# Attention with the keys on the partitions and no row maximum, ahead of a mixture of depths

## The chip, the cores and the metric

The kernel runs on one core of a Trainium2 chip. A core has a matrix engine (TensorE, PE in the rows, with its weight loads as PEld), three engines for elementwise work (VectorE or DVE, ScalarE or ACT, GpSimd or POOL), a queue engine (SyncE or SP) and 16 DMA engines. The metric is the device time of the program in microseconds (us), the median of several runs. All data is float32, for which each matmul of the program is carried out in two passes of the matrix engine; a transpose takes one.

## What is computed

```python
q_n, k_n = rmsnorm(q, g_q), rmsnorm(k, g_k)          # q, k, v: (8, 12, 448, 64)
scores = matmul(q_n, k_n.transpose(0, 1, 3, 2)) / sqrt(64)
attn = exp(scores - max(scores)); attn = attn / (sum(attn) + 1e-9)
x = matmul(attn, v).transpose(0, 2, 1, 3).reshape(8, 448, 768)
# mixture of depths: per batch, the 128 tokens with the highest x @ w_gate
out = x; out[top] += sigmoid(x[top] @ w_gate) * (relu(x[top] @ w1) @ w2)   # w1: 768 x 1024
```

## The kernel before

A batch has 448 tokens; token 4 p + j lies on partition p (112 of them) at place j. The work is cut into units: batch, pair of heads c (six per batch), block j of 112 queries, 192 units in all; four heads are a group, whose q, k and v are loaded three groups ahead (L72, one SP queue). `normalize` (L131) squares a group's q and k on POOL, sums on DVE, takes the power -1/2 on POOL (L144) and scales q and k on POOL (L152). `transpose_pair` (L162) turns q and k of two heads on PE (L170) and multiplies them with g on DVE and ACT.

`scores` (L187) multiplies one block of queries with all keys, queries on the partitions, for two heads whose 64 dims lie on the lower and upper half of the partitions (L193); DVE takes the row maximum from the result (L201), ACT the exponential with its row sum (L206). `transpose_probs` (L216) turns each head's probabilities block by block on PE (L222) and copies them out on DVE and ACT. `values` (L237) multiplies them, now keys on the partitions, with v: the probabilities are the stationary operand and v with its 64 columns the moving one, four blocks of keys per head (L245). DVE divides by the row sums and writes x (L255).

`mixture` (L265) is a generator that yields after each piece. Its pieces run between the units of the next batch: the gate's scores (L276), each token's rank by comparison with all others (L304, L314), a one-hot selection (L354), the gather of the chosen rows by matmuls (L368), the products with w1 (L400) and w2 (L420), and a scattered addition into the output (L433). The mixture of the last batch runs alone at the end.

The loop at L446 sets the order: at step i the scores of unit i, the transposes of unit i - 1, the values of unit i - 2, and one piece of the mixture. The framework's scheduler then orders each engine's queue, and each engine takes its queue strictly in order.

## Time and profile before

| | us |
|---|---|
| median of 3 runs | 1139.58 |
| lowest and highest run | 1129.56, 1142.35 |
| span of the profiled execution | 1137.9 |
| PE busy | 1009.8 (89%) |
| PE weight loads busy | 795.4 (70%) |
| DVE busy | 619.0 (54%) |
| ACT busy | 396.2 (35%) |
| POOL busy | 335.3 (29%) |

The page shows one profiled execution. Matmuls are pipelined, so PE's busy share is not a measure of how near it is to its limit; the spacing of starts in the timeline is. The granted clock is that of PE, 1.00 for 2.4 GHz throughout a stretch.

### The profile page before, as it was taken

The page shows a single profiled execution, that of the slowest core. Times are in us where ns is not written, and L with a number is a line of the kernel's source. Part 1 is how long each engine was busy: PE and PEld are TensorE (multiplying, and loading weights), DVE is VectorE, ACT ScalarE, POOL GpSimd, SP SyncE. Part 2 cuts the span into 40 slices and gives each one's busy share as a digit, 9 for nine tenths or more (in the row PEclk, how much of TensorE's full clock was granted, in tenths as well). Part 3 has the DMA queues.
Part 4 walks back from the last instruction along what each step waited for, and adds up shares of the span by engine and source line. Part 5 has one row for each costly group of instructions (what it writes and reads, how often), then busy time and mean ns, then how long its engine had stood idle before and what let it go on. Part 6 is the DMA issues. An engine that isn't in the chain of part 4 may idle for free.

```text
span 1137.9 us, 17977 instructions
## 1 busy us (share of the span) xinstructions
PE 1009.8 (89%) x7264; PEld 795.4 (70%) x7264; DVE 619.0 (54%) x1379; ACT 396.2 (35%) x1049; POOL 335.3 (29%) x165
## 2 busy tenths in 40 slices
...
DMA packets 37938, 54.98 MB, mean 48 GB/s; under 512 B 1776, under 2 KB 34032, under 8 KB 36960
## 3 DMA queue, kind: packets, MB, share of 16 engines
q1 hardware_dynamic: 36384, 50.68, 15.6%
...
q8 instruction: 58, 0.95, 0.3%
q14 instruction: 24, 0.20, 0.1%
...
## 4 chain that ended last, share of the span: by engine, by line
PE 67%; POOL 21%; DVE 5%; issue 4%; DMA 1%; ACT 1%; POOLq 0%; SPq 0%; ACTq 0%
PE av L245 23%; PE sc L193 13%; PE pt_ps L222 13%; POOL rinv L144 10%; PE moe_ps L420 6%; PE moe_ps L400 4%; POOL sq L138 4%; PE qk_ps L170 4%; PE moe_ps L368 3%; POOL qn L152 3%; POOL kn L152 3%; DVE ss L139 2%; DVE nmax L201 2%; DMA q<-in_q_dram 1%; ACT p L206 1%
## 5 line engine op out<-in xcount | busy, mean ns | idle before, releaser
L245 PE MATMUL av<-v,pt 112*112 112x64 f32 x3072 | 368.7, 276 | 33.6 <-DVE x L255 33.6
L245 PEld LDWEIGHTS av<-v,pt 112*112 112x112 f32 x3072 | 358.1, 195 | 35.4 <-DVE x L255 35.4
L201 DVE TENSOR_REDUCE nmax<-sc 112x2 f32<-112x896 f32 x192 | 208.2, 1085 | 164.3 <-PE sc L193 164.3
L206 ACT ACTIVATE p<-sc,nmax 112x448 f32<-112x448 f32 x384 | 240.0, 632 | 150.4 <-DVE nmax L201 148.1
L222 PEld LDWEIGHTS pt_ps<-ident,p 112*112 112x112 f32 x1536 | 161.6, 143 | 161.5 <-ACT p L206 83.2
L222 PE MATMUL pt_ps<-ident,p 112*112 112x112 f32 x1536 | 207.6, 279 | 48.8 <-ACT p L206 43.0
L231 ACT COPY pt<-pt_ps 112x448 f32<-112x448 f32 x192 | 102.2, 532 | 339.8 <-PE pt_ps L222 339.8
L193 PE MATMUL sc<-kT,qT 64*112 64x448 f32 x768 | 217.2, 642 | 0.0
L229 DVE COPY pt<-pt_ps 112x448 f32<-112x448 f32 x192 | 118.3, 616 | 44.3 <-PE pt_ps L222 44.3
L144 POOL TENSOR_TENSOR rinv<-ss,neg_half 112x32 f32<-112x32 f32 x24 | 134.1, 5589 | 1.6
L152 POOL TENSOR_TENSOR qn<-q,rinv 112x1024 f32<-112x1024 f32 x24 | 49.1, 2046 | 266.8 <-PE qk_ps L170 266.7
L139 DVE TENSOR_REDUCE ss<-sq 112x16 f32<-112x1024 f32 x48 | 58.3, 1215 | 123.8 <-POOL sq L138 123.8
L433 POOL DMA_INDIRECT out_dram<-y,row x8 | 13.1, 1633 | 374.3 <-DVE y L429 374.3
L255 DVE TENSOR_TENSOR x<-av,rden 112x128 f32<-112x128 f32 x192 | 55.6, 289 | 89.8 <-PE av L245 88.9
L400 PE MATMUL moe_ps<-xeT,w 128*128 128x128 f32 x768 | 94.0, 280 | 0.9 <-ACT hT L409 0.7
L400 PEld LDWEIGHTS moe_ps<-xeT,w 128*128 128x128 f32 x768 | 89.8, 195 | 1.2 <-ACT hT L409 0.9
L420 PE MATMUL moe_ps<-w,hT 128*128 128x384 f32 x256 | 89.2, 493 | 1.4 <-DVE y L429 0.7
L193 PEld LDWEIGHTS sc<-kT,qT 64*112 64x112 f32 x768 | 58.1, 187 | 31.5 <-issue 16.7
L206 ACT ACTIVATION_READ_ACCUMULATOR p<-sc,nmax 112x1 f32 x384 | 77.4, 202 | 0.0
L181 ACT ACTIVATE kT<-qk_ps,gk 128x448 f32<-128x448 f32 x48 | 30.4, 633 | 134.0 <-PE qk_ps L170 134.0
L170 PEld LDWEIGHTS qk_ps<-ident,qn 112*128 112x128 f32 x192 | 22.7, 163 | 62.2 <-issue 32.4
L420 PEld LDWEIGHTS moe_ps<-w,hT 128*128 128x128 f32 x256 | 46.3, 190 | 28.2 <-DVE y L429 1.3
...
## 6 DMA issues: line engine op xcount, KB each, us to landing
q<-in_q_dram SPq DMA_DIRECT2D x24, 448.0 KB, 4.4
k<-in_k_dram SPq DMA_DIRECT2D x24, 448.0 KB, 6.7
v<-in_v_dram SPq DMA_DIRECT2D x24, 448.0 KB, 5.8
...
out_dram<-y,row POOLq DMA_INDIRECT x8, 5.6
gq<-in_g_q_dram ACTq DMA_DIRECT2D x2, 0.2 KB, 5.1
```

Source lines behind the costliest of these rows:

```text
L139: nc.vector.tensor_reduce(out=ss[:, i], in_=sq, axis=AX.X, op=OP.add)
L144: nc.gpsimd.tensor_tensor(out=rinv.rearrange(flat), in0=ss.rearrange(flat), in1=neg_half.to_broadcast([CP, 2 * GH * NJ]), op=OP.pow,)
L152: nc.gpsimd.tensor_tensor(out=t.rearrange("p j h d -> p h j d"), in0=loaded.pop((nm, n)), in1=rinv[:, i, :, :, None].to_broadcast([CP, GH, ...
L193: nc.tensor.matmul(out=sc[:, hh, 0:S], lhsT=qT[r, CP * j : CP * (j + 1)], rhs=kT[r, :], start=True, stop=True,)
L201: nc.vector.tensor_reduce(out=nmax, in_=sc[:, :, 0:S], axis=AX.X, op=OP.max, negate=True)
L206: nc.scalar.activation(out=p, in_=sc[:, hh, 0:S], func=AF.Exp, bias=nmax[:, hh : hh + 1], accum_out=den[:, hh : hh + 1],)
L222: nc.tensor.transpose(out=pt_ps[:CP, kc, :], in_=ps[hh][:, CP * kc : CP * (kc + 1)], identity=ident[:CP, :CP],)
L229: nc.vector.tensor_copy(out=pt, in_=pt_ps[:CP])
L231: nc.scalar.copy(out=pt, in_=pt_ps[:CP])
L245: nc.tensor.matmul(out=av[:, hh, :], lhsT=pts[hh][:, kc, :], rhs=loaded["v", b * NG + 2 * c // GH][:, 2 * c % GH + hh, kc, :], start=(kc = ...
L400: nc.tensor.matmul(out=ps[:, 128 * i : 128 * i + n], lhsT=w1[:, dc, 128 * (f0 + i) : 128 * (f0 + i + 1)], rhs=xeT[:, dc, :n], start=(dc == 0),
L420: nc.tensor.matmul(out=ps[:n, : DM // 2], lhsT=hT[:, fc, :n], rhs=w2[:, fc, cols], start=(fc == 0), stop=(fc == NFC - 1),)
```

## The change

The old program becomes the function `general`. A test on the chip forms the largest square of g_q times g_k; if it is at most 3600/64 a branch takes the new function `fast`, else `general`. With rows of q and k divided by their rms, scores can't exceed 60 in that case, so `fast` takes the exponential of the scores without a maximum.

In `fast` the host hands q and k over transposed as well (dims on the partitions), v and the tokens in the order of the partitions. The sum of squares is formed from the token copies (square on ACT, sum on DVE, power on POOL). The factor of k's rows is the scale of the exponential, since keys are on the partitions; the factors of q's rows are stored to DRAM as rows and loaded again onto all partitions (`rows`, `bc`), and `scale_q` multiplies them with q and both g's on DVE.

A unit is now two heads and one block of 112 keys. `scores` gives keys on the partitions and all 448 queries in the columns. `values` uses v as the stationary operand (64 columns for each head, written to the lower or upper 64 partitions of one bank) and the probabilities as the moving one; four units add up to x of two heads, transposed. The sums over keys are added up on DVE (`add_probs`) and finished by four matmuls with ones per group, and x and the sums are turned on PE (`finish_group`). The mixture's pieces are the same; it starts eight units after its batch's end, and the last one runs at the end. `y` has one buffer in place of two.

```diff
+    def load_tokens(n):
+        b, h0 = n // NG, n % NG * GH
+        for i in range(2):
+            t = load_pool.tile([CP, GH, NJ, D], F32, name="tok", bufs=4)
+            nc.sync.dma_start(out=t, in_=tok[b, :, i, h0 : h0 + GH])
+            toks[n, i] = t
+    def load_group(n):
+        b, g = n // NG, n % NG
+        for store, src, name in ((qTs, qT, "qT"), (kTs, kT, "kT")):
+            t = load_pool.tile([128, GH // 2, S], F32, name=name, bufs=2 if name == "qT" else 3)
+            nc.sync.dma_start(
+                out=t, in_=src[b, g * GH // 2 : (g + 1) * GH // 2].rearrange("c p s -> p c s")
+            )
+            store[n] = t
+        t = load_pool.tile([CP, GH, NJ, D], F32, name="v")
+        nc.sync.dma_start(out=t, in_=vp[b, :, g * GH : (g + 1) * GH])
+        vs[n] = t
...
+    def inverse_rms(n):
+        ss = norm_pool.tile([CP, 2, GH, NJ], F32, name="ss")
+        for i in range(2):
+            t = toks.pop((n, i))
+            sq = norm_pool.tile([CP, GH, NJ, D], F32, name="sq", bufs=1)
+            nc.scalar.activation(out=sq, in_=t, func=AF.Square)
+            nc.vector.tensor_reduce(out=ss[:, i], in_=sq, axis=AX.X, op=OP.add)
+            yield
+        rinv = norm_pool.tile([CP, 2, GH, NJ], F32, name="rinv", bufs=5)
+        nc.vector.tensor_scalar(
+            out=ss, in0=ss, scalar1=1.0 / D, scalar2=1e-6, op0=OP.mult, op1=OP.add
+        )
+        flat = "p i h j -> p (i h j)"
+        nc.gpsimd.tensor_tensor(
+            out=rinv.rearrange(flat),
+            in0=ss.rearrange(flat),
+            in1=neg_half.to_broadcast([CP, 2 * GH * NJ]),
+            op=OP.pow,
+        )
+        rinvs[n] = rinv
+        yield
+        rows = dram_pool.tile([GH, S], F32, name="rows")
+        nc.sync.dma_start(
+            out=rows.rearrange("h (p j) -> p h j", j=NJ), in_=rinv[:, 0]
+        )
+        bc = norm_pool.tile([128, GH // 2, S], F32, name="bc")
+        for hh in range(2):
+            src = rows.rearrange("(c hh) s -> hh c s", hh=2)[hh]
+            nc.sync.dma_start(
+                out=bc[D * hh : D * (hh + 1)],
+                in_=dataclasses.replace(src, ap=[[0, D]] + [list(x) for x in src.ap]),
+            )
+        bcs[n] = bc
+        yield
...
+    def scale_q(g):
+        n, c = divmod(g, GH // 2)
+        t = norm_pool.tile([128, S], F32, name="qn", bufs=3)
+        nc.vector.scalar_tensor_tensor(
+            out=t, in0=qTs[n][:, c], scalar=gg, in1=bcs[n][:, c], op0=OP.mult, op1=OP.mult
+        )
+        qns[g] = t
...
+    def scores(u):
+        g, kc = divmod(u, NJ)
+        n, c = divmod(g, GH // 2)
+        p = p_pool.tile([CP, 2, S], F32, name="p")
+        scs = []
+        for hh in range(2):
+            r = slice(D * hh, D * (hh + 1))
+            sc = ps_sc.tile([CP, 512], F32, name="sc")
+            nc.tensor.matmul(
+                out=sc[:, 0:S],
+                lhsT=kTs[n][r, c, CP * kc : CP * (kc + 1)],
+                rhs=qns[g][r, :],
+                start=True,
+                stop=True,
+            )
+            scs.append(sc)
+        for hh in range(2):
+            nc.scalar.activation(
+                out=p[:, hh],
+                in_=scs[hh][:, 0:S],
+                func=AF.Exp,
+                scale=rinvs[n][:, 1, 2 * c + hh, kc : kc + 1],
+            )
+        probs[u] = p
+    def add_probs(u):
+        g, kc = divmod(u, NJ)
+        if kc == 0:
+            return
+        if kc == 1:
+            sums[g] = p_pool.tile([CP, 2, S], F32, name="sum", bufs=3)
+        nc.vector.tensor_tensor(
+            out=sums[g], in0=probs[u - 1] if kc == 1 else sums[g], in1=probs[u], op=OP.add
+        )
...
+    def values(u):
+        g, kc = divmod(u, NJ)
+        n, c = divmod(g, GH // 2)
+        if kc == 0:
+            avs[g] = ps_av.tile([128, 512], F32, name="av")
+        for hh in range(2):
+            nc.tensor.matmul(
+                out=avs[g][D * hh : D * (hh + 1), 0:S],
+                lhsT=vs[n][:, 2 * c + hh, kc, :],
+                rhs=probs[u][:, hh],
+                start=(kc == 0),
+                stop=(kc == NJ - 1),
+            )
+        if kc > 0:
+            probs.pop(u - 1)
+        if kc == NJ - 1:
+            probs.pop(u)
+            t = norm_pool.tile([128, NJ, CP], F32, name="xT", bufs=4)
+            nc.scalar.copy(
+                out=t, in_=avs.pop(g)[:, 0:S].rearrange("d (p j) -> d j p", j=NJ)
+            )
+            xTs[g] = t
...
+    def finish_group(n):
+        b = n // NG
+        ps = ps_aux.tile([128, 512], F32, tag="aux", name="den_ps")
+        for h in range(GH):
+            nc.tensor.matmul(
+                out=ps[32 * h : 32 * (h + 1), 0:S],
+                lhsT=ones,
+                rhs=sums[n * GH // 2 + h // 2][:, h % 2],
+                start=True,
+                stop=True,
+            )
+        for c in range(GH // 2):
+            sums.pop(n * GH // 2 + c)
+        den = norm_pool.tile([128, NJ, CP], F32, name="den", bufs=1)
+        nc.vector.tensor_copy(
+            out=den, in_=ps[:, 0:S].rearrange("d (p j) -> d j p", j=NJ)
+        )
+        yield
+        ps = ps_aux.tile([128, NJ, 128], F32, tag="aux", name="denT_ps")
+        for j in range(NJ):
+            nc.tensor.transpose(out=ps[:CP, j, :], in_=den[:, j, :], identity=ident)
+        rden = norm_pool.tile([CP, NJ, GH], F32, name="rden")
+        nc.vector.reciprocal(
+            out=rden, in_=ps[:CP].rearrange("p j (h r) -> p j h r", r=32)[:, :, :, 0]
+        )
+        yield
+        if b not in xs:
+            xs[b] = x_pool.tile([CP, NJ, DM], F32, name="x")
+        for c in range(GH // 2):
+            g = n * GH // 2 + c
+            t = xTs.pop(g)
+            ps = ps_aux.tile([128, NJ, 128], F32, tag="aux", name="x_ps")
+            for j in range(NJ):
+                nc.tensor.transpose(out=ps[:CP, j, :], in_=t[:, j, :], identity=ident)
+            col = g % NP * 128
+            nc.vector.tensor_tensor(
+                out=xs[b][:, :, col : col + 128].rearrange("p j (h d) -> p j h d", d=D),
+                in0=ps[:CP].rearrange("p j (h d) -> p j h d", d=D),
+                in1=rden[:, :, 2 * c : 2 * c + 2, None].to_broadcast([CP, NJ, 2, D]),
+                op=OP.mult,
+            )
+            yield
...
+    units = B * NP * NJ
+    per_batch = NP * NJ
+    per_group = GH // 2 * NJ
+    LAG = 2
...
+    drain(inverse_rms(0))
+    constants()
+    drain(inverse_rms(1))
+    load_group(1)
+    load_tokens(2)
+    load_weights()
+    scale_q(0)
+    aux, moe, rms = [], iter(()), iter(())
+    for i in range(units + LAG + 1):
+        n, step = divmod(i, per_group)
+        if step == 4:
+            if n + 2 < n_groups:
+                load_group(n + 2)
+            if n + 3 < n_groups:
+                load_tokens(n + 3)
+        if step == 2:
+            drain(rms)
+            rms = inverse_rms(n + 2) if n + 2 < n_groups else iter(())
+        if i < units:
+            scores(i)
+        if i % NJ == 2 and i // NJ + 1 < B * NP:
+            scale_q(i // NJ + 1)
+        if 1 <= i <= units:
+            add_probs(i - 1)
+        if LAG <= i < units + LAG:
+            values(i - LAG)
+            if (i - LAG + 1) % per_group == 0:
+                aux.append(finish_group((i - LAG) // per_group))
+        if i >= LAG + 1 and aux:
+            if next(aux[0], aux) is aux:
+                aux.pop(0)
+        if (i - LAG - 6) % per_batch == 0 and i >= per_batch:
+            while aux:
+                drain(aux.pop(0))
+            drain(moe)
+            moe = mixture((i - LAG - 6) // per_batch - 1)
+        next(rms, None)
+        next(moe, None)
+    while aux:
+        drain(aux.pop(0))
+    drain(moe)
+    drain(mixture(B - 1))
...
+    B, H, S, D = inputs["q"].shape
+    NJ = 4
+    CP = S // NJ
+    a = {name: _np.asarray(inputs[name]) for name in _INS}
+    a["qT"] = a["q"].transpose(0, 1, 3, 2).reshape(B, H // 2, 2 * D, S)
+    a["kT"] = (
+        a["k"].reshape(B, H, CP, NJ, D).transpose(0, 1, 4, 3, 2).reshape(B, H // 2, 2 * D, S)
+    )
+    a["vp"] = a["v"].reshape(B, H, CP, NJ, D).transpose(0, 2, 1, 3, 4)
+    a["tok"] = _np.stack([a["q"], a["k"]], axis=1).reshape(B, 2, H, CP, NJ, D)
+    a["tok"] = a["tok"].transpose(0, 3, 1, 2, 4, 5)
+    a["g2"] = _np.stack([_np.tile(a["g_q"], 2), _np.tile(a["g_k"], 2)], axis=1)
...
+        with tc.tile_pool(name="bound", bufs=1) as pool:
+            g = pool.tile([1, 2, D], F32, name="g")
+            nc.sync.dma_start(out=g[:, 0], in_=ap["g_q"].rearrange("(one d) -> one d", one=1))
+            nc.sync.dma_start(out=g[:, 1], in_=ap["g_k"].rearrange("(one d) -> one d", one=1))
+            prod = pool.tile([1, D], F32, name="prod")
+            nc.vector.tensor_mul(out=prod, in0=g[:, 0], in1=g[:, 1])
+            nc.vector.tensor_mul(out=prod, in0=prod, in1=prod)
+            top = pool.tile([1, 1], F32, name="top")
+            nc.vector.tensor_reduce(out=top, in_=prod, axis=AX.X, op=OP.max)
+            small = pool.tile([1, 1], I32, name="small")
+            nc.vector.tensor_scalar(
+                out=small,
+                in0=top,
+                scalar1=MAX_SCORE * MAX_SCORE / D,
+                scalar2=None,
+                op0=OP.is_le,
+            )
+            is_small = nc.values_load(small[0:1, 0:1], min_val=0, max_val=1,
+                skip_runtime_bounds_check_because="a comparison gives 0 or 1")
+        with tc.If(is_small > 0) as cmp:
+            fast(
+                tc, *(ap[n] for n in ("qT", "kT", "vp", "tok", "g2")),
+                *(ap[n] for n in _INS[5:]), cap, out,
+            )
+        with cmp.Else():
+            general(tc, *(ap[n] for n in _INS), cap, out)
     r = _run(nc, [arrays], core_ids=[0])
```

What stands in PE's order before, around the middle of the program (sc are scores, pt_ps transposed probabilities, av value products, qk_ps transposed q and k):

```order
L245 MATMUL av_3293<-v_1638,pt_3222 112x64 x4
L245 MATMUL av_3293<-v_1638,pt_3229 112x64 x3
L222 MATMUL pt_ps_3279<-ident_109,p_3213 112x112 x4
L222 MATMUL pt_ps_3286<-ident_109,p_3215 112x112 x4
L245 MATMUL av_3293<-v_1638,pt_3229 112x64
L193 MATMUL sc_3321<-kT_3077,qT_3076 112x448 x2
L222 MATMUL pt_ps_3331<-ident_109,p_3261 112x112 x4
L222 MATMUL pt_ps_3338<-ident_109,p_3263 112x112 x4
L245 MATMUL av_3345<-v_2056,pt_3284 112x64 x4
```

And in the changed kernel, from a group's last values on (den_ps are the sums by ones, denT_ps and x_ps the transposes at a group's end):

```order
L242 MATMUL av_1741<-p_1749,v_1253 64x448 x2
L264 MATMUL den_ps_1786<-sum_1613,ones_129 32x448 x2
L264 MATMUL den_ps_1786<-sum_1739,ones_129 32x448 x2
L209 MATMUL sc_1794<-qn_1737,kT_1439 112x448
L209 MATMUL sc_1796<-qn_1737,kT_1439 112x448
L242 MATMUL av_1804<-p_1764,v_1441 64x448 x2
L280 MATMUL denT_ps_1807<-ident_134,den_1791 112x128 x4
L209 MATMUL sc_1819<-qn_1737,kT_1439 112x448
L209 MATMUL sc_1821<-qn_1737,kT_1439 112x448
L242 MATMUL av_1804<-p_1775,v_1441 64x448 x2
L293 MATMUL x_ps_1828<-ident_134,xT_1718 112x128 x4
L209 MATMUL sc_1848<-qn_1800,kT_1439 112x448
```

The transposes between scores and values are gone; a group's denominators and transposes stand between units, one piece after each.

In DVE's order of the changed kernel, at the start of a mixture (cmp are the comparisons for the rank, sum the additions of probabilities, x the products that finish x):

```order
L274 COPY den_4286<-den_ps_4281 128x448
L232 TENSOR_TENSOR sum_4303<-sum_4303,p_4294 112x896
L282 RECIPROCAL rden_4313<-denT_ps_4308 112x16
L345 TENSOR_SCALAR cmp_4322,higher_4320<-moe_ps_4315,gate_4265 112x448
L355 SCALAR_TENSOR_TENSOR cmp_4324,equal_4321<-moe_ps_4315,gate_4265,before_135 112x448
L345 TENSOR_SCALAR cmp_4326,higher_4320<-moe_ps_4315,gate_4265 112x448
L355 SCALAR_TENSOR_TENSOR cmp_4328,equal_4321<-moe_ps_4315,gate_4265,before_135 112x448
L345 TENSOR_SCALAR cmp_4347,higher_4320<-moe_ps_4315,gate_4265 112x448
L295 TENSOR_TENSOR x_4340<-x_ps_4341,rden_4313 112x4x128
L355 SCALAR_TENSOR_TENSOR cmp_4349,equal_4321<-moe_ps_4315,gate_4265,before_135 112x448
L345 TENSOR_SCALAR cmp_4351,higher_4320<-moe_ps_4315,gate_4265 112x448
L355 SCALAR_TENSOR_TENSOR cmp_4353,equal_4321<-moe_ps_4315,gate_4265,before_135 112x448
```

Comparisons of a mixture stand between a group's reciprocal, its x products and the additions.

In SP's order at the start (tok are the token copies, rows and bc the way of the factors through DRAM):

```order
L87 DMA tok_119<-in_tok_dram 112x1024
L87 DMA tok_121<-in_tok_dram 112x1024
L177 DMA rows_150<-rinv_147 112x4x4
L94 DMA qT_183<-in_qT_dram 128x2x448
L94 DMA kT_185<-in_kT_dram 128x2x448
L183 DMA bc_152<-rows_150 64x2x448 x2
L177 DMA rows_178<-rinv_175 112x4x4
L99 DMA v_187<-in_vp_dram 112x1024
L87 DMA tok_189<-in_tok_dram 112x1024
L183 DMA bc_180<-rows_178 64x2x448 x2
L87 DMA tok_191<-in_tok_dram 112x1024
```

Each group's bc stands behind its rows and behind loads of the next group.

## Rows read from the trace of the kernel before

**Rows 1.** The page, part 1: busy us, share of the span, instructions.

```profile
PE 1009.8 (89%) x7264; PEld 795.4 (70%) x7264; DVE 619.0 (54%) x1379; ACT 396.2 (35%) x1049; POOL 335.3 (29%) x165
```

**Rows 2.** The page, part 4: the chain that ended last, shares by line.

```profile
PE av L245 23%; PE sc L193 13%; PE pt_ps L222 13%; POOL rinv L144 10%; PE moe_ps L420 6%; PE moe_ps L400 4%; POOL sq L138 4%; PE qk_ps L170 4%; PE moe_ps L368 3%; POOL qn L152 3%; POOL kn L152 3%; DVE ss L139 2%; DVE nmax L201 2%; DMA q<-in_q_dram 1%; ACT p L206 1%
```

**Rows 3.** Timeline, PE, from 904 us: start, us, instruction, [idle before].

```profile
904.33 1.01 PE L193 MATMUL sc<-kT,qT 64*112 64x448 f32 x4
905.27 0.98 PE L222 MATMUL pt_ps<-ident,p 112*112 112x112 f32 x8
906.09 1.70 PE L245 MATMUL av<-v,pt 112*112 112x64 f32 x16
907.62 2.90 PE L400 MATMUL moe_ps<-xeT,w 128*128 128x128 f32 x24
910.45 1.01 PE L193 MATMUL sc<-kT,qT 64*112 64x448 f32 x4
```

**Rows 4.** The same view, the last w2 products.

```profile
1124.78 5.43 PE L420 MATMUL moe_ps<-w,hT 128*128 128x384 f32 x16 [0.71 <-DVE y L429]
```

**Rows 5.** Timeline, all engines, the first scores.

```profile
30.58 2.89 PE L193 MATMUL sc<-kT,qT 64*112 64x448 f32 x8
```

**Rows 6.** Timeline, all engines, the last value products.

```profile
1084.26 1.79 PE L245 MATMUL av<-v,pt 112*112 112x64 f32 x16 [0.38 <-DVE x L255]
```

**Rows 7.** Stretches: busy us of each engine, granted clock, DMA share, GB/s.

```profile
30.00:100.00 70.00, 55.66 (x290) 41.37 (x292) 34.52 (x59) 21.13 (x57) 47.45 (x23) 0.67 0.47 150
...
400.00:500.00 100.00, 88.45 (x660) 71.59 (x660) 61.57 (x140) 37.52 (x101) 40.22 (x19) 0.88 0.23 60
...
900.00:1000.00 100.00, 99.40 (x783) 77.81 (x782) 63.06 (x150) 44.79 (x119) 11.45 (x6) 1.00 0.07 19
```

**Rows 8.** Waits, all engines: us in total, times, longest.

```profile
PE pt_ps L222 <- ACT p L206: 43.0, 13, 10.1
```

**Rows 9.** Timeline, PE, a place where one head's scores stand alone.

```profile
86.92 1.00 PE L193 MATMUL sc<-kT,qT 64*112 64x448 f32 x2
```

**Rows 10.** Timeline from 502.8 us: the last w1 pass, then a unit's scores.

```profile
502.83 0.28 PE L400 MATMUL moe_ps<-xeT,w 128*128 128x128 f32 x1
...
503.03 1.01 PE L193 MATMUL sc<-kT,qT 64*112 64x448 f32 x4
```

**Rows 11.** The page, part 5, ACT: busy us, mean ns, idle before.

```profile
L206 ACT ACTIVATE p<-sc,nmax 112x448 f32<-112x448 f32 x384 | 240.0, 632 | 150.4 <-DVE nmax L201 148.1
...
L231 ACT COPY pt<-pt_ps 112x448 f32<-112x448 f32 x192 | 102.2, 532 | 339.8 <-PE pt_ps L222 339.8
...
L206 ACT ACTIVATION_READ_ACCUMULATOR p<-sc,nmax 112x1 f32 x384 | 77.4, 202 | 0.0
```

**Rows 12.** Groups of instructions of DVE and POOL, shapes apart, columns as before.

```profile
L201 DVE TENSOR_REDUCE nmax<-sc 112x2 f32<-112x896 f32 x192 | 208.2, 1085 | 164.3 <-PE sc L193 164.3
...
L144 POOL TENSOR_TENSOR rinv<-ss,neg_half 112x32 f32<-112x32 f32 x24 | 134.1, 5589 | 1.6
L229 DVE COPY pt<-pt_ps 112x448 f32<-112x448 f32 x192 | 118.3, 616 | 44.3 <-PE pt_ps L222 44.3
...
L139 DVE TENSOR_REDUCE ss<-sq 112x16 f32<-112x1024 f32 x48 | 58.3, 1215 | 123.8 <-POOL sq L138 123.8
...
L276 DVE SCALAR_TENSOR_TENSOR prod<-x,wg 112x768 f32<-112x768 f32 x32 | 30.6, 955 | 0.9
...
L177 DVE TENSOR_SCALAR qT<-qk_ps,gq 128x448 f32<-128x448 f32 x48 | 32.4, 675 | 7.2 <-PE qk_ps L170 7.2
```

**Rows 13.** The page, parts 3 and 6: a DMA queue; loads, KB, us to landing.

```profile
q1 hardware_dynamic: 36384, 50.68, 15.6%
...
k<-in_k_dram SPq DMA_DIRECT2D x24, 448.0 KB, 6.7
...
gq<-in_g_q_dram ACTq DMA_DIRECT2D x2, 0.2 KB, 5.1
```

**Rows 14.** Waits of SP's queue: us in total, times, longest.

```profile
SPq L79 <- POOL qn L152: 790.6, 21, 51.2
```

284 lines of the change are left out of this document (272 added, 12 removed).

## The prediction

> **What bounds the kernel now.** I read the page first: TensorE (PE) has work for 89% of the span, VectorE (DVE) for 54%, ScalarE (ACT) for 35% [rows 1], and in the chain that ended last the value products, the scores and the transposes of the probabilities are the largest lines [rows 2]. A busy share says little where matmuls are pipelined, so I went to the timeline at a place without idle time. A unit (two heads, 112 queries) takes there: scores 0.94 us (904.33 to 905.27), eight transposes 0.82 (to 906.09), sixteen value passes 1.53 (to 907.62), then a piece of the mixture, 24 passes in 2.83 [rows 3]. A pair's q and k are eight transposes too, so 0.82. So PE alone needs 192 x 3.29 = 632 us for the units, 48 x 0.82 = 39 for q and k, and about 28.6 for one mixture: 144 passes of w1 and of the gather at 2.83/24 = 0.118 us (17.0), 32 passes of w2 at 5.43/16 = 0.34 at most (10.6, [rows 4]), small ones 1.0. With seven mixtures between units (200) that is 871 us. The stretch from the first score to the last value product is 30.6 to 1086.1 = 1055 us [rows 5, 6]. The 184 us between them are idle time and a lower clock, about in equal parts: one stretch of 100 us has PE busy 88.5 us at a granted clock of 0.88, another 99.4 at 1.00 [rows 7]. The longest waits of PE itself are for the softmax [rows 8].
>
> The profiled span is 1137.9 us, the median of the runs 1139.6, so the sum below is made against the span and needs no correction.
>
> **The change on PE.** Per unit the 8 transposes, their two evacuations and the 16 short value passes go; the 48 q/k transposes go too. With the keys on the partitions, the exponentials are already the moving operand of the value product, v is stationary, and one matmul per head has 448 columns in place of 64. A float32 matmul is two passes.
> - Scores: the same shape as now, 0.94 us per unit, 192 x 0.94 = 180 us.
> - Values: two heads, each 112 x 64 stationary, outputs on partitions 0 to 63 and 64 to 127, two passes of 448 columns each. No row has this form. The nearest for one head alone is w2: 384 columns in 5.43/16 = 0.34, less the last pass's tail about 0.33 [rows 4], so 448 columns take 0.385, and four in series 1.54 + 0.1 for the change of shape = 1.64 us. The nearest for two heads that use different parts of the array is the scores: four passes take 1.01 us from first start to last end [rows 3], and where one head's two passes stand alone they take 1.00 [rows 9]. Two heads on different halves cost what one costs. I take the scores' 0.94 for the values also: 180 us. The lower bound is the same without its two edges of 0.09 (next but one), 0.76.
> - These products use halves of the array's columns, the scores halves of its rows. The Trainium skill, TensorEngine Tiling (Array Packing), Key Properties, says that tiles work independently, and its section When to Use Tiling lists just this exchange of stationary and moving operand for narrow results. By that page the values would cost 0.76 to 0.94 and the sum below come to 771 us or less; by the row of one head alone it would be 938. No run so far shows column halves.
> - A change of shape costs: after the mixture's passes at 0.118 the scores start 0.20 us after the last one's start (502.83 to 503.03) [rows 10], about 0.09 more. The 0.94 holds both edges of a score burst, and I charge 0.1 for each further burst. The same page (Key Properties) says that a change of tiling mode drains the engine, which speaks against a kernel that alternates two modes 384 times; charged once more per unit (0.1 x 192) it would add 19 us, 790 in all. The trace agrees that there is an edge, with the 0.09 us above, and I go by the row.
> - Denominators: a group of four heads sums its probabilities on DVE, then four matmuls with 32 columns of ones, 448 columns each, into four quarters. Two-by-two logic as above: 0.94 per group, 24 x 0.94 = 23 us; in series 8 x 0.385 + 0.1 = 3.2.
> - Twelve transposes per group with 128 columns: 288 x 0.118 = 34, and 72 bursts x 0.1 = 7.
> - Mixture unchanged: 7 x 28.6 = 200, in some 16 pieces, 7 x 16 x 0.1 = 11.
>
> Sum of PE: 180 + 180 + 23 + 34 + 7 + 200 + 11 = 635 us.
>
> **ACT and DVE.** ACT loses the accumulator reads (77.4 us), the copies of the transposed probabilities (102.2) and the kT copies; it keeps 384 exponentials at 0.63 at most [rows 11], and gains 48 squares of 1024 elements (0.53 for a copy of 448 elements, so 1.2 at most) and 48 copies of xT: 242 + 58 + 26 and little for the mixture, 330 us or 1.7 per unit against 1.9 on PE, with the mixture's PE work on top. Scores of a unit and its values lie two units apart in the PE order, 3.7 us, and two exponentials need 1.2, so they are covered; without that cover each unit would cost 1.2 more.
> DVE loses the row maximum (208 us), half the copies (118) and small work per unit. It gains 144 additions of 896 elements (1.09 by the reduction of 896 elements), 48 scalings of q (0.68), 24 evacuations (0.62) and 48 products of 512 elements (0.75); the 48 sums of squares stay at 1.22 [rows 12]. Per group 6.5 + 2.4 + 1.4 + 0.6 + 1.5 + 0.4 = 12.8, times 24 = 307. A mixture has four gate products (0.96) and eight comparisons (0.62, as a copy of 448 elements) and some 4 us of small ones, 13, times 8 = 104. That is 411 us: below PE in total, not at the start of each mixture. The comparisons start there when PE has turned the gate's row, 3.7 us after the group's denominators (0.9 + 1.9 + 0.5 + 0.4), and with two x products, an addition and the picks (about 1.0) they take 5.0 + 1.5 + 1.1 + 1.0 = 8.6: to 12.3 us. PE has scores, values and transposes until 11.3 (3.7 + 3 x 1.9 + 2 x 0.5 + 0.94) and then stands before the gather. It waits 1 to 3 us. I take 2 x 7 = 14 us.
>
> **The clock.** So far idle time and clock loss are about equal, so 14 more. The first stretch after the head runs at 0.67 [rows 7], where each unit waits for its softmax. Here nothing makes PE wait then; 10 us for warming up and filling.
>
> **Head and tail.** Now the first score starts at 30.6 [rows 5]. In the changed kernel a small load (5.1 us, as gq [rows 13]), five short DVE instructions (0.8) and a branch (in no row; 0 to 5, I take 2) come first: 5.1 + 0.8 + 2 = 7.9. Then tok (6.7 for the second, as k [rows 13]), one square and one reduction (1.2 each), the power (5.6 [rows 12]), the store of its rows (16 bytes each, priced as gq at 5.1), the broadcast load (about 5.5) and one scaling (0.7): 33.9. The broadcast stands behind qT and kT on SP's queue, so 37. The tail from the last value product is 1137.9 - 1086.1 = 52 us now [rows 6]. It keeps the last mixture and gets the last group's closing (sum 1.1, denominators 0.9, copy 0.6, twelve transposes 1.4, a reciprocal 0.2, two products 1.5, waits of 0.1 between them: 6.5) and three more of the 0.96-us gate products, which now can start only when x is whole: 61.
>
> **DMA.** 24 groups x (5 x 448 KB + 0.46 MB) + out and weights is near 87 MB. The queue moved 50.7 MB in 15.6% of the span, 178 us [rows 13], so 87 need 305 us of 770. Loads are issued a group ahead and more; a late one would cost about 5 us.
>
> **Sum.** 37 + 635 + 61 + 14 + 14 + 10 = 771, so 770 us.
>
> **The rivals.**
> - *Columns in series.* If the halves of the columns don't overlap, values cost 0.70 more per unit (134) and denominators 2.3 more per group (54); the DVE wait goes under that with some clock, about 20. 770 + 188 - 20 = 938 us. For it: no row shows column halves together. Against: the scores do it by rows. Chance 0.15.
> - *DVE decides more than the mixtures' starts.* If an addition costs 1.9 us (nothing shows it; 896 elements in 1.09 speaks against it) DVE has some 530 us of work, the bursts cost 8 us more each and every group's denominators wait about a microsecond: 56 + 24 = 80, 850 us. Chance 0.08.
> - *The rows' way through memory is exposed; slower.* Squares, sum, power, store and broadcast are some 22 us in series. If each group's chain starts only when the last group ends, since SP waits in order (it waited 790.6 us for POOL now [rows 14]), 23 x 22 = 506 us come on top: 1276. It ends slower than now from 16 us per group. Against: the order issues rows and broadcasts of a group at least one group (about 17 us or more) ahead. Chance 0.03.
> - *The branch takes the general path.* Then the old work runs behind the test: 1138 + 9 = 1147. The inputs have a largest |g_q g_k| of 5.26 and the test lets up to 7.5 through. Chance 0.02.
>
> **How the numbers follow.** My forecast, halves of columns together and PE the limit, has 0.72; its own range is 705 (edges cheaper, 0.76 per burst, some 66 us less) to 845 (two times the waits and a clock of 0.9, as now). The whole range must take in the serial case, so 705 to 955, which leaves out under 2 in 10. About 1% is what a measurement can tell from no change. Faster by over 1%: 0.72 + 0.15 + 0.08 = 0.95; the general path by 1147 is within 1%, 0.02; slower 0.03.
>
> **What would show it.** Values' matmuls of two heads starting some 10 ns apart, about 0.94 us per unit, some 180 us in all (over 300 if in series); a granted clock of 0.95 or more between 100 and 650 us; waits of PE for DVE only around picks and denominators; first score near 37 us; some 61 us from the last value product to the end. A unit of over 2.5 us without a mixture piece, or PE waiting for qn, would make the forecast wrong.

## The result, and the profile after the change

The changed kernel takes 808.75 us, median of four runs (805.47 to 811.77), against 1136.01 for the kernel before in the same comparison: a ratio of 0.711, with a 95% interval of 0.707 to 0.715. The forecast was 770. The time lies in the forecast's range and in the own range of its likeliest case, 39 us above the value. The profiled execution has a span of 810.0 us, and the forecast's sum is held against that.

The page of the changed kernel, parts 1 (busy us), 2 (the clock granted to PE, in tenths, over 40 slices), 3 (the queue of the loads) and 4 (the chain that ended last, by engine and by line):

```profile
PE 703.0 (87%) x3520; PEld 333.3 (41%) x3520; DVE 389.7 (48%) x690; ACT 307.7 (38%) x521; POOL 156.3 (19%) x44
...
PEclk9999789998889979899899997899999999999588
...
q1 hardware_dynamic: 43300, 83.89, 37.8%
...
PE 51%; issue 16%; POOL 10%; DVE 9%; DMA 8%; ACT 4%; SPq 2%; POOLq 0%; ACTq 0%; DVEq 0%
```

PE's passes are halved from [rows 1], 7264 to 3520, and its busy time fell by 307 us. GpSimd (POOL) has 10% of the chain, all of it its power; the power had 10% before too [rows 2].

The timeline of PE from 484.7 us is the place to compare with [rows 3]:

```profile
484.71 1.01 PE L209 MATMUL sc<-qn,kT 64*112 64x448 f32 x4
485.65 0.97 PE L242 MATMUL av<-p,v 112*64 112x448 f32 x4
486.55 0.96 PE L264 MATMUL den_ps<-sum,ones 112*32 112x448 f32 x8
489.76 2.36 PE L209 MATMUL sc<-qn,kT 64*112 64x448 f32 x4 [2.25 <-ACT p L218]
492.05 1.76 PE L242 MATMUL av<-p,v 112*64 112x448 f32 x4
...
495.32 1.84 PE L209 MATMUL sc<-qn,kT 64*112 64x448 f32 x4
```

Scores take 0.94 us a unit (484.71 to 485.65), values 0.90 (to 486.55), and eight passes of four heads' denominators about as much. Then PE stands for 2.25 us, and behind that the same scores take 2.3 us (489.76 to 492.05), the next ones 1.84 where they took 1.01 to their last end, and the same values 1.76.

The stretches of the changed kernel, columns as in [rows 7]:

```profile
40.00:100.00 60.00, 53.19 (x226) 14.99 (x224) 34.92 (x44) 35.56 (x61) 20.38 (x4) 0.91 0.91 266
100.00:200.00 100.00, 89.36 (x452) 41.39 (x448) 56.48 (x97) 46.10 (x75) 30.94 (x7) 0.95 0.61 149
200.00:300.00 100.00, 90.44 (x446) 42.13 (x444) 50.64 (x88) 39.16 (x67) 19.99 (x4) 0.91 0.40 106
300.00:400.00 100.00, 90.64 (x446) 42.08 (x444) 48.86 (x87) 38.17 (x65) 19.61 (x4) 0.91 0.39 105
400.00:500.00 100.00, 91.24 (x452) 42.41 (x452) 50.29 (x88) 39.33 (x67) 19.98 (x4) 0.93 0.37 101
500.00:600.00 100.00, 94.96 (x488) 43.27 (x488) 54.38 (x97) 41.21 (x72) 22.95 (x5) 0.96 0.36 99
600.00:700.00 100.00, 99.59 (x535) 46.70 (x533) 54.26 (x114) 41.67 (x76) 5.36 (x2) 1.00 0.23 60
700.00:747.00 47.00, 47.00 (x266) 26.64 (x268) 12.05 (x17) 13.11 (x24) 0.96 (x1) 1.00 0.00 1
```

Read PE's busy time (the first number after the comma) and the granted clock (third from the right). Added over the rows, PE is idle for 50.6 us (6.8 + 10.6 + 9.6 + 9.4 + 8.8 + 5.0 + 0.4), and what the clock is below 1.00, times the length, comes to 39 us (5.4 + 5 + 9 + 9 + 7 + 4). The two overlap: by the trace's records the clock is at its lower level for 78.5 us, and for 14.2 of these PE is idle anyway. PE works at half speed for 64.3 us and loses half of them, 32 us. The last 147 us have neither: hardly any normalisation is left to do, and GpSimd has 6 us of work in them.

The waits of the changed kernel (us in total, times, longest) that lie on this:

```profile
POOL rinv L167 <- ACT p L218: 264.9, 10, 32.7
...
ACT sq L159 <- DVE ss L160: 73.9, 23, 7.7
...
DVE ss L160 <- POOL rinv L167: 55.0, 12, 5.3
...
PE denT_ps L280 <- DVE den L274: 27.8, 13, 5.0
...
PE sc L209 <- ACT p L218: 15.0, 7, 4.4
```

PE waits for the copy of the denominators on VectorE and for exponentials on ScalarE (and once, 5.7 us at 107 us, for VectorE's products of x), and these stand in queues behind an instruction of the normalisation. The timeline of all engines shows one of these places:

```profile
508.47 5.84 POOL L167 TENSOR_TENSOR rinv<-ss,neg_half 112x32 f32<-112x32 f32 x1 [17.96 <-DVE sum L232]
...
511.66 0.96 PE L264 MATMUL den_ps<-sum,ones 112*32 112x448 f32 x8
...
514.35 1.22 DVE L160 TENSOR_REDUCE ss<-sq 112x16 f32<-112x1024 f32 x1 [3.28 <-POOL rinv L167]
...
515.60 1.06 ACT L159 ACTIVATE sq<-tok 112x1024 f32<-112x1024 f32 x1 [3.77 <-DVE ss L160]
...
516.56 1.14 ACT L218 ACTIVATE p<-sc,rinv 112x448 f32<-112x448 f32 x2
...
518.83 0.62 DVE L274 COPY den<-den_ps 128x448 f32<-128x448 f32 x1
...
519.50 1.10 PE L280 MATMUL denT_ps<-ident,den 128*112 128x128 f32 x4 [5.04 <-DVE den L274]
```

Read it downward. The power of group 20 (groups counted from 0) starts at 508.47, when the last exponential of group 15 (508.33) has freed one of five rinv tiles; the row names an addition that ended shortly before, ten other powers name the exponential itself. It ends at 514.31. Only then does one of the two ss tiles come free, and VectorE, which has stood for 3.28 us at the reduction of group 22, goes on. The square (L159) waits for that reduction, since there is one sq tile, and the exponentials wait behind the square. The copy of the denominators (L274), due since 512.62, runs at 518.83 behind two reductions, and PE's transpose starts at 519.50 after 5.04 us without work. These reductions are for a group that PE comes to six groups later. The loop writes them two groups ahead; the order that the scheduler made of it runs them as far ahead as tiles allow, and there the two engines stand at them.

### The profile page after: what moved, and what is told of

It reads as the page before. It is cut to its first block, busy times and chain, and to the rows that moved or that the text cites. A ratio compares the mean times of both kernels' runs of the same rounds, so it can differ in the third digit from the quotient of the medians.

```text
span 810.0 us, 9106 instructions
## 1 busy us (share of the span) xinstructions
PE 703.0 (87%) x3520; PEld 333.3 (41%) x3520; DVE 389.7 (48%) x690; ACT 307.7 (38%) x521; POOL 156.3 (19%) x44
## 3 DMA queue, kind: packets, MB, share of 16 engines
q1 hardware_dynamic: 43300, 83.89, 37.8%
## 4 chain that ended last, share of the span: by engine, by line
PE 51%; issue 16%; POOL 10%; DVE 9%; DMA 8%; ACT 4%; SPq 2%; POOLq 0%; ACTq 0%; DVEq 0%
PE sc L209 13%; PE av L242 11%; POOL rinv L167 10%; PE moe_ps L461 8%; PE moe_ps L441 7%; DMA tok<-in_tok_dram 7%; PE moe_ps L409 5%; DVE ss L160 4%; ACT sq L159 3%; PE x_ps L293 2%; DVE sum L232 2%; PE denT_ps L280 1%; ACT p L218 1%; PE den_ps L264 1%; DMA rows<-rinv 1%
## 5 line engine op out<-in xcount | busy, mean ns | idle before, releaser
L218 ACT ACTIVATE p<-sc,rinv 112x448 f32<-112x448 f32 x384 | 223.2, 630 | 252.9 <-PE sc L209 230.4
L209 PE MATMUL sc<-qn,kT 64*112 64x448 f32 x768 | 219.3, 618 | 47.4 <-DVE qn L194 32.3
L167 POOL TENSOR_TENSOR rinv<-ss,neg_half 112x32 f32<-112x32 f32 x24 | 139.4, 5809 | 437.8 <-ACT p L218 264.9
L242 PE MATMUL av<-p,v 112*64 112x448 f32 x768 | 197.9, 591 | 0.0
L232 DVE TENSOR_TENSOR sum<-sum,p 112x896 f32<-112x896 f32 x96 | 104.6, 1090 | 73.0 <-ACT p L218 72.4
L209 PEld LDWEIGHTS sc<-qn,kT 64*112 64x112 f32 x768 | 60.4, 181 | 136.1 <-ACT p L218 66.3
L242 PEld LDWEIGHTS av<-p,v 112*64 112x64 f32 x768 | 39.9, 139 | 137.6 <-issue 131.0
L159 ACT ACTIVATE sq<-tok 112x1024 f32<-112x1024 f32 x48 | 50.8, 1059 | 100.3 <-DVE ss L160 73.9
L232 DVE TENSOR_TENSOR sum<-p 112x896 f32<-112x896 f32 x48 | 52.2, 1088 | 68.8 <-ACT p L218 68.8
L409 PE MATMUL moe_ps<-pick,x 112*128 112x128 f32 x384 | 51.5, 295 | 6.3 <-DVE pick L395 5.6
L409 PEld LDWEIGHTS moe_ps<-pick,x 112*128 112x128 f32 x384 | 48.4, 207 | 16.7 <-issue 6.6
L474 POOL DMA_INDIRECT out_dram<-y,row x8 | 13.7, 1718 | 204.5 <-DVE y L470 204.3
L280 PE MATMUL denT_ps<-ident,den 128*112 128x128 f32 x96 | 19.2, 334 | 28.1 <-DVE den L274 27.8
L293 PEld LDWEIGHTS x_ps<-ident,xT 128*112 128x112 f32 x192 | 20.5, 139 | 45.8 <-DVE x L295 14.2
```

The lines of the kernel that those rows point to most:

```text
L159: nc.scalar.activation(out=sq, in_=t, func=AF.Square)
L167: nc.gpsimd.tensor_tensor(out=rinv.rearrange(flat), in0=ss.rearrange(flat), in1=neg_half.to_broadcast([CP, 2 * GH * NJ]), op=OP.pow,)
L209: nc.tensor.matmul(out=sc[:, 0:S], lhsT=kTs[n][r, c, CP * kc : CP * (kc + 1)], rhs=qns[g][r, :], start=True, stop=True,)
L218: nc.scalar.activation(out=p[:, hh], in_=scs[hh][:, 0:S], func=AF.Exp, scale=rinvs[n][:, 1, 2 * c + hh, kc : kc + 1],)
L232: nc.vector.tensor_tensor(out=sums[g], in0=probs[u - 1] if kc == 1 else sums[g], in1=probs[u], op=OP.add)
L242: nc.tensor.matmul(out=avs[g][D * hh : D * (hh + 1), 0:S], lhsT=vs[n][:, 2 * c + hh, kc, :], rhs=probs[u][:, hh], start=(kc == 0), stop=(k ...
```

## The experiments

All times are medians; each ratio is to runs of the kernel before that were taken along with it. "Middle" is first score to last value product in the profiled execution, "idle" PE's idle time in it, "half" the time of it at the lower of the two clock levels, both added up from the trace's records. "Work" is the middle less idle, less half of PE's busy time at the lower level: what the middle would take with PE always busy at the full clock.

| kernel | us | ratio to before, 95% | middle | idle | half | work |
|---|---|---|---|---|---|---|
| changed | 808.75 | 0.711 (0.707 to 0.715) | 715.0 | 50.8 | 78.5 | 632.0 |
| e1_no_power | 744.95 | 0.660 (0.657 to 0.662) | 651.0 | 17.9 | 3.4 | 631.4 |
| e2_more_buffers | 769.30 | 0.682 (0.679 to 0.685) | 674.6 | 29.5 | 30.7 | 633.5 |
| e3_no_ties | 795.81 | 0.705 (0.701 to 0.708) | 703.2 | 51.7 | 64.9 | 625.8 |
| e4_serial_values | 915.85 | 0.810 (0.805 to 0.814) | 823.7 | 28.0 | 58.0 | 768.7 |
| e5_ss_only | 781.75 | 0.691 (0.685 to 0.696) | 686.4 | 34.9 | 44.4 | 633.4 |
| e6_power_twice | 840.31 | 0.742 (0.735 to 0.748) | 741.7 | 73.7 | 105.8 | 629.9 |
| e7_late_weights | 775.79 | 0.687 (0.680 to 0.694) | 677.8 | 31.0 | 34.1 | 631.6 |
| e8_no_branch | 802.65 | 0.708 (0.702 to 0.714) | 715.6 | 53.0 | 64.9 | 635.6 |
| e9_newton | 749.41 | 0.664 (0.660 to 0.668) | 656.5 | 19.3 | 13.7 | 630.3 |
| e10_newton_buffers | 746.91 | 0.661 (0.658 to 0.664) | 656.0 | 18.9 | 10.2 | 632.0 |
| e11_rinv_only | 786.37 | 0.697 (0.693 to 0.700) | 692.7 | 40.5 | 51.2 | 632.8 |

PE's work is 630 to 636 us in all of them but e3 and e4, so what sets these kernels apart in the middle is idle time and the clock.

Theory A says that GpSimd's power, through the sums of squares, holds the queues of VectorE and ScalarE and by them PE. Theory B says that VectorE's own work at the mixtures' starts, the forecast's term of 14 us, is larger than priced.

**The power replaced by a copy.**

```diff
-        nc.gpsimd.tensor_tensor(
-            out=rinv.rearrange(flat),
-            in0=ss.rearrange(flat),
-            in1=neg_half.to_broadcast([CP, 2 * GH * NJ]),
-            op=OP.pow,
+        nc.gpsimd.tensor_scalar(
+            out=rinv, in0=ss, scalar1=1.0, scalar2=None, op0=OP.mult
```

> The power -1/2 on POOL (5.8 us for each group) is left out: rinv is the mean square itself, taken over by a 0.2-us POOL instruction, so rows are not normalized; the order of all instructions on PE, DVE and ACT stays word for word. Theory A (the power holds the sums of squares on DVE, which hold copies and additions behind them, and PE with them): PE's two stalls in each batch, 2.25 and 5.04 us, go, idle time between first score and last value product falls from 50 to about 15 us, the half-clock time after each stall from 78 to about 25 us, and the head is 5.6 us shorter: 735 to 750 us. Theory B (the burst of comparisons at a mixture's start holds PE, as the prediction had it): only the head's 5.6 us: about 803 us, stalls in their places.

64 us went by the medians; between the two profiled spans it is 72, of which 64 in the middle, 6 in the head and 2 in the tail. What is left of the waits (line numbers are three lower there), and a stretch:

```profile
PE denT_ps L277 <- DVE den L271: 9.6, 7, 1.7
...
PE sc L206 <- ACT p L215: 1.8, 2, 1.6
```

```profile
200.00:300.00 100.00, 97.38 (x530) 47.74 (x528) 58.30 (x111) 44.29 (x76) 4.54 (x4) 1.00 0.41 112
```

VectorE's waits for GpSimd are down from 3.3 to 5.3 us each to 0.18 us, four times, and the clock stays up. That is theory A: the power alone is worth more than the 39 us by which the forecast missed.

**More tiles for the sums and the roots, the work whole.**

```diff
-        ss = norm_pool.tile([CP, 2, GH, NJ], F32, name="ss")
+        ss = norm_pool.tile([CP, 2, GH, NJ], F32, name="ss", bufs=8)
-        rinv = norm_pool.tile([CP, 2, GH, NJ], F32, name="rinv", bufs=5)
+        rinv = norm_pool.tile([CP, 2, GH, NJ], F32, name="rinv", bufs=12)
```

> The work is whole; ss has 8 buffers in place of 2 and rinv 12 in place of 5, so a sum of squares needn't wait until the power of two groups earlier has read its tile, and a power not until the exponentials of five groups earlier are done. PE's order stays, DVE's and ACT's change in a few places. Theory A: the stalls go without the power being left out, 745 to 765 us. Theory B: 805 to 812 us.

39 us are gained, a little less than theory A's range. VectorE's wait for GpSimd is no row any more, and the stretches show when the waits end:

```profile
200.00:300.00 100.00, 90.50 (x466) 42.27 (x460) 57.80 (x100) 47.01 (x78) 27.45 (x6) 0.97 0.48 128
300.00:400.00 100.00, 99.65 (x528) 44.66 (x524) 55.15 (x103) 42.69 (x78) 20.85 (x4) 1.00 0.41 111
```

From 300 us on PE has work without a gap. What is left lies before 240 us.

**One half of it each.** e5_ss_only has the change of the ss tiles alone, e11_rinv_only that of the rinv tiles.

> Of the two buffer counts changed together in e2_more_buffers (sums of squares 2 to 8, inverse roots 5 to 12; 769.3 us) only the first is changed here; PE's and POOL's orders are those of the changed kernel, row for row. Theory A, the sums of squares hold VectorE up: a reduction of tokens has no free ss tile until GpSimd has raised the one two groups earlier to its power, and the additions and the copy of the denominators stand behind it in VectorE's queue. Then ss alone gives nearly all: 765-778 us, and no wait of VectorE for GpSimd's rinv among the waits. Theory B, the inverse roots hold it up (GpSimd's powers wait up to 32.7 us each for the exponentials to free one of five rinv tiles, and are late by that): then the powers stay late, and the time stays within 800-812 us.

> The other half of e2_more_buffers: inverse roots 5 to 12, sums of squares left at 2. e5_ss_only gave 781.75 us and both together 769.3. Theory A, the ss tile is what VectorE waits for, and the root tiles only what makes the powers late once that is gone: alone they give nothing or a little, 800-811 us, with VectorE still waiting for GpSimd's rinv. Theory B, the two act apart and add up: 12.5 us less than the changed kernel, 793-798 us.

The first and the second half alone gave 27 and 22 us, where both together give 39; neither time lies in any range that was given for it. The row of waits in the two kernels, e5_ss_only first:

```profile
DVE ss L160 <- POOL rinv L167: 26.4, 6, 5.3
```

```profile
DVE ss L160 <- POOL rinv L167: 18.4, 5, 5.3
```

The counts explain both. A reduction may run ahead of the exponentials by the rinv tiles plus the ss tiles: 5 + 2 = 7 groups, 5 + 8 = 13, 12 + 2 = 14, 12 + 8 = 20. In the changed kernel the lead is used up when group 12 is to be reduced (194 us), and the twelve groups from there to 23 wait, once each; with 13 it is group 18, and six wait; with 14 groups 20 to 23 wait, and a short one of 1.4 us stands at group 15; with 20 none before the work is over. The starts in the traces bear this out: the reductions that wait run 6 groups ahead of PE's scores in the changed kernel, 12 in e5 and 13 in e11, one less than the count, since a release comes with a group's last exponential. Each wait taken away is worth 3.2 to 4.5 us (39/12, 27/6, 22/7), idle time and the low clock behind it. So it is one chain with two stores of tiles in it, and more of either only moves the point where the queue stops. How long it stops is the power's doing: e1, with the counts of the changed kernel and a copy in the power's place, runs its reductions as far ahead and waits 0.18 us where this one waits 3.3 to 5.3.

**The power done twice.**

```diff
+        spare = norm_pool.tile([CP, 2, GH, NJ], F32, name="spare")
+        nc.gpsimd.tensor_tensor(
+            out=spare.rearrange(flat),
+            in0=ss.rearrange(flat),
+            in1=neg_half.to_broadcast([CP, 2 * GH * NJ]),
+            op=OP.pow,
+        )
```

> The changed kernel with a second power of the same size on GpSimd ahead of each of the 24, into a tile that nobody reads; nothing else is added. A power takes 5.6-6.2 us. Theory A, GpSimd's power sits in a chain that TensorE waits for in each of batches 2 to 5, two waits a group (2.25 and 5.04 us now): each of some 8 to 14 waits grows by up to 5.8 us, 45-80 us more in waits, and the stretches at half clock behind them grow or stay, so 845-900 us. Theory B, the powers are ahead of need by a whole group, and what TensorE waits for is VectorE's own work: GpSimd is busy 156 us of 810 and would be busy some 295, with room for it, 805-815 us. If neither, the writing order that the added instruction shifts is worth looking at first.

32 us more: outside of B's range, and short of A's. The waits of 2.25 and 5.0 us in the later batches did not grow at all; the waits that grew stand before 200 us: 10.1 us at 94 and 11.5 at 120, each a power longer than in the changed kernel (4.4 at 86 and 5.7 at 107). The timeline of GpSimd there says why:

```profile
512.52 6.32 POOL L174 TENSOR_TENSOR rinv<-ss,neg_half 112x32 f32<-112x32 f32 x1 [22.95 <-ACT p L225]
...
522.81 5.45 POOL L168 TENSOR_TENSOR spare<-ss,neg_half 112x32 f32<-112x32 f32 x1 [0.30 <-DVE ss L163]
539.20 5.87 POOL L174 TENSOR_TENSOR rinv<-ss,neg_half 112x32 f32<-112x32 f32 x1 [10.94 <-ACT p L225]
```

The spare power needs no rinv tile and was over (528.3) while GpSimd waited for one until 539.2. One power lies behind each release, whether GpSimd does one or two; before the lead is used up (the first 200 us) the powers stand in series and count in full. This was the refinement that theory A lacked: it is the release of a tile that starts the power, and the power's 5.8 us are what VectorE then waits for, less what it has still to do.

**Half of the comparisons left out.**

```diff
-            nc.vector.scalar_tensor_tensor(
-                out=cmp,
-                in0=row_ps[:CP, 0:S],
-                scalar=sc[:, j : j + 1],
-                in1=before[:, j].rearrange("p a r -> p (a r)"),
-                op0=OP.is_equal,
-                op1=OP.mult,
-                accum_out=equal[:, j : j + 1],
-            )
```

> Four of the eight comparisons of each mixture are left out (those that rank tokens with equal scores), 4 x 0.68 = 2.7 us of DVE just ahead of the picks. Theory B: the wait of PE at each mixture's start gets shorter by up to 2.7 us and the clock's loss behind it by as much: 7 x 5 = 35, and 2.7 in the tail: about 770 us. Theory A: the stalls stay, only the tail's 2.7 us and the 0.5 to 1.1 us gaps change: 800 to 806 us.

13 us less, more than theory A's range allows, of which 4 in the tail (63.2 to 59.2 us). The waits of 2.25 and 5.04 us stand where they stood, in all four batches, and idle time in the middle is the same (51.7). So theory B does not explain them. Of the 12 us of the middle 6 go with a shorter time at the low clock (PE works 51.5 us in it, against 64.3). The other 6 are PE's work, and the order of its queue shows them. In the changed kernel, once in each of the seven mixtures, the gather's passes stand between the two heads of a unit's scores:

```profile
611.68 1.00 PE L209 MATMUL sc<-qn,kT 64*112 64x448 f32 x2
612.75 2.94 PE L409 MATMUL moe_ps<-pick,x 112*128 112x128 f32 x24
615.63 1.00 PE L209 MATMUL sc<-qn,kT 64*112 64x448 f32 x2
```

Each head alone then takes what both take together ([rows 9] showed that), 1.07 and 0.93 us (to 616.56) in place of 0.94: about 1 us a mixture. With four comparisons fewer the four passes stand together in all seven. So the comparisons did cost PE something at the mixtures' starts, by the order and not by a wait.

**Values in series.** The two heads' v become one stationary tile of 128 columns, so that the four passes cannot use separate halves; each head's probabilities meet both heads' values there.

```diff
-                out=avs[g][D * hh : D * (hh + 1), 0:S],
-                lhsT=vs[n][:, 2 * c + hh, kc, :],
+                out=avs[g][:, 0:S],
+                lhsT=vs[n][:, c, kc, :],
```

> Both heads' v stand side by side as one stationary tile of 128 columns (the host lays them so), and each head's product goes over all 128 columns into the same bank, so four passes of 448 columns per unit can't overlap; x then holds sums over both heads. If halves of the columns overlap and that is worth 0.70 us per unit, as the rival in series was priced, values take 1.6 us per unit and the time is 808 + 134 less what this hides of the stalls, 915 to 942 us. If a unit's time is set by something else than the passes, 808 us.

The timeline of PE in this kernel:

```profile
484.48 1.01 PE L209 MATMUL sc<-qn,kT 64*112 64x448 f32 x4
485.42 1.77 PE L242 MATMUL av<-p,v 112*128 112x448 f32 x4
487.03 0.60 PE L293 MATMUL x_ps<-ident,xT 128*112 128x128 f32 x4
```

Four passes take 1.61 us (485.42 to 487.03) against 0.90 with column halves. 0.71 x 192 units are 136 us, and the middle grew by 109: idle time fell by 23 us and the half clock's loss by 5, as the chain behind the power has more time to hide.

**The weights loaded later.** e2_more_buffers with the three loads moved to step 14 of the loop.

```diff
-    load_weights()
...
+        if i == 14:
+            load_weights()
```

> e2_more_buffers (769.3 us) with the three weight loads (6.3 MB) issued in step 14 of the loop instead of ahead of it; the first product that reads the gate's row comes at about 121 us, the first that reads w1 at 152 us. e2's waits that are left stand nearly all between 84 and 230 us: 4.78 us at 84.5, 5.47 at 105.7, 5.09 at 204.8, with the squares of tokens on ScalarE waiting for their transfers (6.16 and 5.47 us at 81 and 101), and the DMA engines 0.8 to 1.0 busy from 40 to 140 us. Theory A, the tokens' transfers lie behind the weights' on the same engines, so with the weights later the stalls of 84 and 105 us go: about 10 us of waits and 10-14 us of half clock less, 740-757 us. Theory B, the bytes are the same and the engines are near full up to 140 us either way: the waits move to the transfers that now collide with the weights, 764-775 us, or more if the first mixture comes to wait for w1.

Not faster (the intervals of e7 and e2 overlap). The waits of 4.78 and 5.47 us at 84 and 105 us became one of 4.70 at 53 and one of 4.02 at 109, with a square that waits for its tokens again:

```profile
56.25 1.06 ACT L159 ACTIVATE sq<-tok 112x1024 f32<-112x1024 f32 x1 [6.71 <-DMA tok<-in_tok_dram]
```

The waits moved with the loads, as B had it; the time is 1 us above B's range.

**No test, no branch.**

```diff
-        with tc.If(is_small > 0) as cmp:
-            fast(
+        fast(
...
-        with cmp.Else():
-            general(tc, *(ap[n] for n in _INS), cap, out)
```

> The changed kernel without the test of the bound and without the branch: the gains aren't looked at, the path without row maximum is run directly, and the general path isn't in the program. What is left out is the decision, so this kernel is right only for gains within the bound. The prediction priced test and branch at 7.9 us in front of the first score; the trace of the changed kernel shows the token loads issued at 4.26 us, with the gains landed by 2.7 us and four VectorE instructions to 3.6. Theory A, they cost what the trace shows in the head, 3-5 us, and nothing later: 803-806 us. Theory B, a branch around a long program also costs in the loop (code loading): 795 us or less. Theory C, it is hidden behind the first loads: 808-811 us.

6 us less by the medians; the ratios' intervals overlap, so the head is the better witness. Its first score is at 25.4 us against 31.8, and ScalarE loads its table there before the tokens come:

```profile
1.24 1.28 ACT L159 ACT_TABLE_LOAD   x1 [1.24 <-PEq L1008]
```

The middle is the same (715.6 to 715.0), so nothing is lost in the loop.

**Another inverse root.** VectorE computes it in eleven instructions (my expectation said twelve): a first guess from the exponent's bits, and three Newton steps.

```diff
+        nc.vector.tensor_scalar(
+            out=half, in0=ss.bitcast(I32), scalar1=1, scalar2=None, op0=OP.logical_shift_right
+        )
+        nc.vector.tensor_scalar(
+            out=rinv.bitcast(I32), in0=half, scalar1=-1.0, scalar2=float(0x5F3759DF),
+            op0=OP.mult, op1=OP.add,
+        )
+        for _ in range(3):
+            step = norm_pool.tile([CP, 2, GH, NJ], F32, name="step")
+            nc.vector.tensor_mul(out=step, in0=rinv, in1=rinv)
+            nc.vector.scalar_tensor_tensor(
+                out=step, in0=step, scalar=-0.5, in1=ss, op0=OP.mult, op1=OP.mult
+            )
+            nc.vector.scalar_tensor_tensor(
+                out=rinv, in0=step, scalar=1.5, in1=rinv, op0=OP.add, op1=OP.mult
+            )
```

> The whole work with another inverse root: in place of GpSimd's power (5.6 us) twelve small instructions of VectorE on 112x32 (a shift, a subtraction for the first guess, three Newton steps of three), 0.12 to 0.18 us each by the row of L163's 112x32 instruction (0.118 to 0.185), some 1.4-2.2 us a group and 34-52 us of VectorE in all. Buffers are those of the changed kernel. Theory A, the delay of the sums of squares comes from GpSimd's power: with the chain 3.5-4 us shorter and on one engine, no reduction waits for a free ss tile, and the time comes near e1_no_power's 744.95 us: 745-765. Theory B, VectorE is the engine that is late, and what is added to its queue stands in front of the additions and the copies of the denominators: 775-810 us.

> e9_newton with e2_more_buffers' counts (ss 8, inverse roots 12). If theory A of e9_newton holds, the buffers have nothing left to hide: within 8 us of e9_newton. If VectorE's own queue is what is late, the buffers give some of their 12-40 us again.

749.41 us with the whole work and the changed kernel's tiles, 59 less, and the extra tiles then add nothing that the intervals tell apart. The page of e9_newton, part 1, and PE's waits:

```profile
PE 676.0 (90%) x3520; PEld 324.0 (43%) x3520; DVE 428.0 (57%) x954; ACT 309.4 (41%) x521; POOL 15.6 (2%) x20
```

```profile
PE denT_ps L291 <- DVE den L285: 8.9, 7, 2.0
```

VectorE has 38 us more work and PE waits for it less, 8.9 us at the denominators against 27.8. The reductions run six groups ahead here too, with the same 5 and 2 tiles; what is gone is the wait for another engine behind each release. Both e9_newton and e10_newton_buffers do the whole computation and beat both kernels.

## Why the prediction was right, and where its sum was off

- **Column halves overlap; the rival of columns in series is out.** Values measured 0.90 us a unit where 0.94 was taken, denominators about 0.9 a group. The alternating stationary forms cost no more than the edges charged. The Trainium skill, TensorEngine Tiling (Array Packing), Key Properties, says that tiles work independently: the trace agrees, 0.90 us beside 1.61 in series. The Trainium skill, in the same section, has a change of tiling mode drain the engine, for which I had weighed 19 us; the trace shows no more than the edge inside the 0.90.
- **PE's work was right.** 715.0 less 50.8 idle less 32 for the clock is 632 us; the sum had 635. The values took 8 less (192 x 0.04), and the scores that the gather parts took some 6 more, which the sum had not. (At the lower end of the forecast's own range the cheaper edges are priced at 66 us; 384 bursts of 0.18 are 69.)
- **Head and tail nearly right, by terms that cancel.** First score at 31.8 for 37, tail 63.2 for 61. In the head:

```profile
1.20 0.22 SPq L1022 DMA_DIRECT2D g<-in_g_k_dram  x1
...
2.72 0.21 DVE L1026 TENSOR_TENSOR prod<-g 1x64 f32<-1x64 f32 x1 [2.72 <-DMA g<-in_g_k_dram]
...
4.26 0.79 SPq L87 DMA_DIRECT2D tok<-in_tok_dram  x2
...
8.53 1.28 ACT L159 ACT_TABLE_LOAD   x1 [8.53 <-DMA tok<-in_tok_dram]
...
20.25 0.33 SPq L177 DMA_DIRECT2D rows<-rinv  x1
...
22.82 1.32 SPq L183 DMA_DIRECT2D bc<-rows  x2
...
30.99 1.28 DVE L194 SCALAR_TENSOR_TENSOR qn<-qT,gg,bc 128x448 f32<-128x448 f32 x2 [9.93 <-DMA bc<-rows]
```

  The gains landed 1.5 us after their issue (1.20 to 2.72), not 5.1, and the rows were through in 2.6, not 5.1; the broadcast took 8.2, not 5.5. Test and branch together cost 6.4 us by e8 (priced 7.9): 3.5 by the later loads (4.26 against 0.80 there), 1.3 by a table load of ScalarE that stands behind the first tokens here and at 1.24 us, in front of them, in e8, and the rest in a broadcast that lands later.
- **The step that failed is the one on waits and clock: 14 + 14 + 10 = 38 us predicted, 50.8 + 32 = 83 measured.** Those 45 us, less 3 in PE's work, less 5 in the head, plus 2 in the tail, are the 39. I sized the waits from VectorE's list of work at a mixture's start and put them before the gather. No wait of PE there is in the trace but the tail's one; PE waits before the scores and before the denominators' transposes. One of the forecast's own signs of being wrong is there too, a unit of over 2.5 us without a mixture's piece: 4.1 us from 489.76, at the lower clock. That the time still lies in the own range is owed to that range's width: its end of 845 allowed for twice the waits and a clock of 0.9, for no cause that was named. "Nothing makes PE wait then" held for the data of the softmax and not for the engines' queues: an exponential waits when the square ahead of it in ScalarE's order waits, and that one for VectorE, and that one for GpSimd.
- **I looked at the chain of squares, sum, power and rows, and priced only its far end.** The rival of its exposure asked whether rows and broadcasts come in time for their group. They nearly always do: PE waits for qn at the start and once more, 0.6 us at 71 us. But the early work ties up the queues just because it is early. The power's 10% of the chain stood in [rows 2] and its 5589 ns in [rows 12]; the numbers of ss and rinv tiles, 2 and 5, stood in the code and entered no line of the sum.
- **The rival "VectorE decides" named the right place for a wrong reason.** It charged about a microsecond to each group's denominators; 27.8 us were lost there in all. Its cause, a slow addition, is out: an addition of 896 elements takes 1090 ns, the 1.09 of the sum.
- **Loads and the other engines.** VectorE has 389.7 us of work for 411 forecast, ScalarE 307.7 for 330, the load queue 83.9 MB in 37.8% of 810, 306 us for 305. The branch took the short path. Busy time was well priced everywhere; the order of the queues was not.
- **Clock.** Forecast 0.95 or more between 100 and 650 us; 200 to 500 has 0.91 to 0.93. I had taken the clock's loss to be as large as the idle time; it is 32 to 50.8, about six tenths. It was the waits that were too few.

The Trainium skill, Perfetto Trace Analysis, Optimization Strategy, says that the same gap repeating on the engine that should be full can mean too few tiles. The trace agrees: 2.25 and 5.04 us return in each of four batches, and tiles alone (e2) removed them from 240 us on. The faster inverse root (e9) removed them with the tiles as they are.

What stays open is the way to the waits before 240 us that e2 keeps (4.8, 5.5 and 5.1 us the longest). e7 showed only that moving the weights does not help. The power has a part in them: twice the power made the changed kernel's two long waits there a power longer each (e6), and without a power on GpSimd PE's longest wait between 40 us and the last value product is 2.6 us in e9 and 2.8 in e10, which has e2's tiles. The squares there wait for their tokens, up to 5.8 us in the changed kernel and up to 2.6 in e9. SP's queue is a likely link: a group's rows leave it when the power ends (86.29 and 86.32 us), and token loads stand behind them (88.18). No run changed that order alone.
